# Threshold attention and a bilinear FFN: products in 128x64 array tiles rewritten as four 64x64 tiles

## The chip, the cores and the metric

One NeuronCore of a Trainium2 chip runs the whole program. The time is the device time of one execution in microseconds (us). The engines are PE (TensorE, matmul; PEld is its weight load), DVE (VectorE), ACT (ScalarE), POOL (GpSimd) and SP (SyncE, which here only issues DMAs). Matmuls write PSUM, eight banks of 128 partitions x 512 fp32 values; DVE and ACT carry results from there to SBUF.

## The reference

All arrays are fp32 but the weights w_a, w_b and w_out, which come as fp64. B = 8 batches, H = 8 heads, S = 576 positions, D = 64; the FFN has 4608 rows, a width of 512 and an inner width of 1536.

```
scores = q @ k.T / sqrt(64)                      # (8, 8, 576, 576)
thresh = max(scores, -1) - tau                   # tau = 0.02
scores = where(scores >= thresh, scores, -1e9)
attn   = exp(scores - max(scores, -1))
attn   = attn / (sum(attn, -1) + 1e-9)
o      = attn @ v                                # (8, 8, 576, 64)
x      = o.transpose(0, 2, 1, 3).reshape(4608, 512)
out    = ((x @ w_a) * (x @ w_b)) @ w_out         # (4608, 512)
```

## The kernel before

Heads are taken in pairs (32 pairs; the first head on partitions 0 to 63, the second on 64 to 127). A pair has five *units*: four of 128 queries for each of the two heads (u = 0 to 3) and one with the last 64 queries of both (u = 4, called NT). The loop over g (160 units, and three more rounds for what lags) writes out an order for every engine; `keep_order` at the end makes it binding. Each engine therefore does its work strictly in the order in which the loop issues it.

For one unit the loop issues, in this order:

1. `scores` (L308): PE multiplies qT by kT into two PSUM tiles of two banks each (`ps_sc`). qT and kT hold one head on each half of the partitions, so the two heads' products are two 64-row tiles of the array (64*128 in the profile: rows * columns). For u = NT a helper tile `q_diag` holds both heads' 64 queries with zeros elsewhere, written by POOL, and the product goes through `halves`, two tiles of 128 rows and 64 columns (128*64). DVE then takes the row maximum (L317), POOL the bias and threshold (L318, L319).
2. `turn_back`: SP fetches transposed weights of an older unit from a scratch in DRAM (wT).
3. `turn_blocks` for the unit before: DVE transposes in blocks of 32 (L398), SP writes them to the scratch. The first eight units are turned on PE instead (`turn_pe`, with PSUM tiles tp).
4. `weigh`: ACT takes exp (L330), DVE compares, multiplies and sums (L334).
5. `reciprocal` on DVE (L347), `normalise` on ACT (L353).
6. `advance(SPLIT * pace)`: a part of the FFN, see below.
7. every few units `weighted`: the product pv of attention weights and v for 256, 320 or 64 queries (`product`, L449), which lags three units behind. It has five slots of 128 keys; the fifth is shared by the two heads and uses `v_diag`, a tile with zeros written by POOL. ACT copies pv to the tile xT (L479, L487).
8. `advance((1 - SPLIT) * pace)`.

The FFN works on blocks of 256 rows, 18 of them. `ffn` is a generator: for each of 12 slices of 128 inner columns it makes two accumulation chains on PE, x @ w_a and x @ w_b (both called pab, four matmuls of 128 rows deep, each as two 128*64 tiles by `halves`, L457). ACT copies the first to a tile `a` (L517), DVE multiplies `a` with the second to h (L521). Then for each 128 of the 256 rows a chain po of 12 matmuls of 512 columns; ACT copies it to osb (L532) and SP stores it. In the profile each fp32 matmul is two records.

`advance` counts columns: it goes on with the generator until the pace of this unit is used up. Pace grows with the backlog of blocks (CATCH_UP). pv's columns are charged to the same account.

PSUM: four of eight banks are `ps_sc`, the other four are `ps_1`, a pool of four tiles of one bank that pab, po, pv and tp take in turn. A chain can start only when the tile that it takes has been read out.

SBUF: x blocks and raw fp64 weights share the tag xT (six tiles), h has twelve tiles. Weights are converted from fp64 to fp32 in 36 pieces of 128x512 in the first 160 us, spread over ACT, DVE and POOL.

Of the kernel before, what the change touches and what calls it, by code (L numbers as in the profile page):

```python
# [24 lines left out]
XT_BUFS = 6  # L25
W_BUFS = 4
WT_BUFS = 2
A_BUFS = 2
H_BUFS = 12
# [4 lines left out]
PACE_EARLY = 0.04  # L34

# [15 lines left out]
def kernel(  # L51
# [69 lines left out]
    ps_1 = pool("ps_1", 4, space=PSUM)  # L121
# [33 lines left out]
    wa_sb = const.tile([P, HP, DFF], FP32, name="wa_sb")  # L155
    wb_sb = const.tile([P, HP, DFF], FP32, name="wb_sb")
    wo_sb = const.tile([P, NF, DM], FP32, name="wo_sb")
    CW = DM
    pieces = []
    for f0 in range(0, DFF, CW):  # L160
        for c in range(HP):
            for dst, src in ((wa_sb, w_a), (wb_sb, w_b)):
                pieces.append((dst[:, c, f0:f0 + CW], src[c * P:(c + 1) * P, f0:f0 + CW]))
    for F in range(NF):
        pieces.append((wo_sb[:, F, :], w_out[F * P:(F + 1) * P, :]))
    NPIECES = len(pieces)
    raws, stages = {}, {}
    state = {"loaded": 0, "converted": 0, "rows": 0, "shared": 0}

    def load_weights(limit, engine=nc.sync):  # L170

        while len(raws) < limit and state["loaded"] < NPIECES:
            n = state["loaded"]
            raw = work.tile([P, CW, 2], U32, tag="xT", bufs=XT_BUFS, name="raw")
            engine.dma_start(raw.rearrange("p f w -> p (f w)"), pieces[n][1].bitcast(U32))
            raws[n] = raw
            state["loaded"] = n + 1
# [68 lines left out]
    q_diag = [const.tile([P, P], FP32, name=f"q_diag{i}") for i in range(1)]  # L246
    v_diag = [const.tile([P, 2, D], FP32, name=f"v_diag{i}") for i in range(2)]
    shared = []
    for t in q_diag + v_diag:
        nc.gpsimd.memset(t, 0.0)  # L250
# [15 lines left out]
    blocks, swaps, ready = [], {}, []  # L266
# [8 lines left out]
    def prep_pe(i, name):  # L275
# [3 lines left out]
        tps = []  # L279
        for c in range(2):  # L280
            tp = ps_1.tile([P, SH], FP32, tag="ps1", name="tp")
            for n in range(NR // 2):
                nc.tensor.transpose(tp[:, n * R:(n + 1) * R], m[:, c * (NR // 2) + n], ident[0:R, 0:R])
            tps.append(tp)
        prepared.setdefault(i, {})[name] = mT
        return mT, tps

    def prep_copy(mT, tps):
        for c, tp in enumerate(tps):
            nc.vector.tensor_copy(mT[:, c * SH:(c + 1) * SH], tp)  # L290

    def prep_tail(i):

        qT, qd = prepared[i]["q"], q_diag[0]
        for j in range(2):
            r = slice(j * D, (j + 1) * D)
            nc.gpsimd.tensor_copy(qd[r, j * TAIL:(j + 1) * TAIL], qT[r, MAIN:S])

    def scores(i, u):
        qT, kT = prepared[i]["q"], prepared[i]["k"]  # L300
        qd = q_diag[0]
        n = 2 if u < NT else 1
        sc = [ps_sc.tile([P, 2, 512], FP32, tag="sc", name="sc")[:, :, 0:SH] for _ in range(n)]
        for c in range(2):
            for j in range(n):
                if u < NT:
                    r = slice(j * D, (j + 1) * D)
                    nc.tensor.matmul(sc[j][:, c], qT[r, u * P:(u + 1) * P],  # L308
                                     kT[r, c * SH:(c + 1) * SH], start=True, stop=True)
                else:  # L310
                    halves(sc[j][:, c], qd, kT[:, c * SH:(c + 1) * SH], True, True)
# [51 lines left out]
    def turn_pe(i, u):  # L363
# [3 lines left out]
        turned[i, u, "pe"] = wT  # L367
        for j, w in enumerate(ws):
            tp = ps_1.tile([P, NT, P], FP32, tag="ps1", name="tp")
            for s in range(NT):  # L370
                c = TAIL * j + s * P
                nc.tensor.matmul(tp[:, s, :], w[:, c:c + P], dg[:, j], start=True, stop=True)
            nc.scalar.copy(wT[:, 5 * j:5 * j + NT], tp)
        tp = ps_1.tile([P, P], FP32, tag="ps1", name="tp")
# [15 lines left out]
    def turn_blocks(i, u):  # L390
# [20 lines left out]
        else:  # L411
            tb = work.tile([P, NB, Q], FP32, tag="tbt", bufs=1, name="tbt")
# [21 lines left out]
    def shared_slot(i):  # L434

        vm, vd = loaded[i]["v"], v_diag[state["shared"] % 2]
        state["shared"] += 1
        for j in range(2):
            r = slice(j * D, (j + 1) * D)
            nc.gpsimd.tensor_copy(vd[r, j], vm[r, NT])  # L440
        shared.append(vd)

    def product(wT, vm, n):
        vd = shared.pop(0)
        pv = ps_1.tile([P, n], FP32, tag="ps1", name="pv")
        for s in (NT, 0, 1, 2, 3):
            for j in range(2):
                k0 = NT if s == NT else 5 * j + s
                nc.tensor.matmul(pv[j * D:(j + 1) * D], vd[:, j] if s == NT else vm[:, k0], wT[:, k0, :],  # L449
                                 start=(s == NT), stop=(s == NT - 1))  # L450
        return pv

    def halves(out, stationary, moving, start, stop):

        for c in range(2):
            r = slice(c * D, (c + 1) * D)
            nc.tensor.matmul(out[r], stationary[:, r], moving, start=start, stop=stop)  # L457

    def weighted_unit(i, u):
# [5 lines left out]
        nc.scalar.copy(x_of[b, 0][:, hp, u * P:(u + 1) * P], pv)  # L465
        if hp == HP - 1:
            state["rows"] = u + 1
            if u == 0:
                blocks.append((x_of[b, 0], ("first", b, 0)))

    def weighted(i, h):
# [4 lines left out]
        if h < 2:  # L476
            if hp == 0:
                x_of[b, h] = work.tile([P, HP, HALF], FP32, tag="xT", bufs=XT_BUFS, name="xT")
            nc.scalar.copy(x_of[b, h][:, hp, :].rearrange("p (t i e) -> p i t e", t=2, e=Q),  # L479
                           pv[:, 0:HALF].rearrange("p (i t e) -> p i t e", t=2, e=Q))  # L480
            if hp == HP - 1:
                blocks.append((x_of.pop((b, h)), ("half", b, h)))
        if n % HALF:
# [3 lines left out]
            nc.scalar.copy(xtail_of[b // GT][:, hp, t * TAIL:(t + 1) * TAIL], pv[:, n - TAIL:n])  # L487
            del loaded[i], prepared[i]
            if hp == HP - 1 and t == GT - 1:
                blocks.append((xtail_of.pop(b // GT), ("tail", b - t, 0)))  # L490


    def ffn(xT, what):


        kind, b, h = what
        hs = []
        steps = [(F, 0, HALF) for F in range(NF)]
        if kind == "first":
            n = CW // P  # L500
            steps = [(F, c, c + P) for c in (0, P) for F in range(n)] + steps[n:]
        for F, c0, c1 in steps:
            while (state["converted"] < 2 * HP * (F * P // CW + 1)
                   or kind == "first" and state["rows"] * P < c1):
                yield 0
            fs = slice(F * P, (F + 1) * P)
            pab = []
            for w in (wa_sb, wb_sb):
                p = ps_1.tile([P, c1 - c0], FP32, tag="ps1", name="pab")
                for c in range(HP):  # L510
                    halves(p, w[:, c, fs], xT[:, c, c0:c1], c == 0, c == HP - 1)
                    if c < HP - 1:
                        yield c1 - c0
                pab.append(p)
                if w is wa_sb:
                    a = work.tile([P, c1 - c0], FP32, tag="a", bufs=A_BUFS, name="a")
                    nc.scalar.copy(a, p)  # L517
                    yield c1 - c0
            if c0 == 0:
                hs.append(work.tile([P, HALF], FP32, tag="h", bufs=H_BUFS, name="h"))  # L520
            nc.vector.tensor_tensor(hs[F][:, c0:c1], a, pab[1], op=ALU.mult)  # L521
            yield c1 - c0
        for u in range(2):
            po = ps_1.tile([P, DM], FP32, tag="ps1", name="po")
            for F in range(NF):
                while state["converted"] < NPIECES - NF + F + 1:
                    yield 0
                halves(po, hs[F][:, u * P:(u + 1) * P], wo_sb[:, F, :], F == 0, F == NF - 1)
                if F < NF - 1:
                    yield DM  # L530
            osb = work.tile([P, DM], FP32, tag="osb", bufs=OSB_BUFS, name="osb")
            nc.scalar.copy(osb, po)  # L532
# [7 lines left out]
            yield DM  # L540
# [169 lines left out]
```

## Time and profile before

| | |
|---|---|
| three runs | 1590.07, 1589.36, 1590.07 us; median 1590.07 |
| the profiled execution | 1591.21 us, of it 1589.4 us span |
| PE matmul records / weight loads | 11696 / 11696 |
| pab L457, 128x256 (all forms together) | 7040 records |
| po L457, 128x512 | 1728 records, 383.7 us |
| sc L308, 64x288 | 1024 records, 165.6 us |
| sc L457 on q_diag, 128x288 | 256 records, 36.5 us |
| pv L449 | 1440 records |
| ACT copy a, 128x256 (L517) | x212, mean 362 ns |
| ACT copy osb, 128x512 (L532) | x36, mean 570 ns |
| DVE h, 128x256 / 128x128 (L521) | x212, mean 416 ns / x8, mean 275 ns |
| POOL copies v_diag / q_diag | 34.4 / 14.9 us |
| DMA, instructions | 92 packets, 1.51 MB (queue q8) |
| swap<-tb, 288 KB; out, 256 KB: issue to landing | 5.1; 3.6 us (median) |

The busy times of engines are shares of the whole span and add up over stages with different limits. A matmul record lasts longer than its turn on the array, since matmuls are pipelined; the time that one costs is read from the distance of two starts. "Idle before" and its releaser tell what ended a wait.

### The profile page before, as it was taken

What the parts mean: (1) busy time and instruction counts of PE and PEld (TensorE: products, weight loads), DVE (VectorE), ACT (ScalarE), POOL (GpSimd) and SP (SyncE); (2) the same over time, 40 slices, a digit from 0 to 9 for tenths busy, and PEclk for the clock granted to TensorE, in tenths of its full rate; (3) what the DMA queues carried; (4) which work ended last, traced back from release to release, by engine and by line L of the source; (5) the groups of instructions that cost most, each with busy time, mean ns of one, the idle gap of its engine ahead of it and who ended that gap; (6) DMA issues with size and microseconds to landing.
All of it is one profiled execution on the core that took longest, in us unless ns stands there. A gap on an engine that the chain in (4) does not pass through costs nothing.

```text
span 1589.4 us, 29502 instructions
## 1 busy us (share of the span) xinstructions
PE 1523.8 (96%) x11696; PEld 852.8 (54%) x11696; DVE 828.3 (52%) x1810; ACT 592.3 (37%) x1045; POOL 250.3 (16%) x737
## 2 busy tenths in 40 slices
PE   6879999998999999999999999999999999999998
PEld 4655454644646464645555555555464546464654
DVE  6787465556655665564444654466545655430100
ACT  5766344433433443343332333343433333320010
POOL 4766111111111111110111111111101111000000
PEclk9989999999999999999999999999999999999999
DMA  9458877678767875785636956488656865550000
GB/s 226 156 144 221 168 139 175 142 150 185 170 150 145 183 177 132 148 173 129 141 82 123 186 128 143 104 181 163 145 108 148 181 149 133 111 127 14 1 14 14
DMA packets 621018, 218.99 MB, mean 138 GB/s; under 512 B 542544, under 2 KB 611664, under 8 KB 620880
## 3 DMA queue, kind: packets, MB, share of 16 engines
q1 hardware_dynamic: 618512, 216.52, 61.5%
q8 instruction: 92, 1.51, 0.4%
q10 hardware_dynamic: 2368, 0.59, 0.2%
q14 instruction: 46, 0.38, 0.1%
HBM read 127.40 MB, written 89.65 MB: 137 GB/s over the span
## 4 chain that ended last, share of the span: by engine, by line
PE 82%; DVE 6%; issue 3%; ACT 3%; DMA 3%; SPq 2%; POOL 1%; DVEq 0%; POOLq 0%; ACTq 0%
PE pab L457 41%; PE po L457 21%; PE pv L449 9%; PE sc L308 8%; PE sc L457 2%; DVE mx L317 1%; DVE w L334 1%; DMA wT<-swap 1%; SPq L137 1%; DVE tb L398 1%; ACT w L353 1%; SPq L420 1%; SPq L408 1%; POOL bias L318 1%; DMA km<-in_k_dram 1%
## 5 line engine op out<-in xcount | busy, mean ns | idle before, releaser
L317 DVE TENSOR_REDUCE mx<-sc 128x1 f32<-128x576 f32 x288 | 206.0, 752 | 379.1 <-PE sc L308 317.0
L457 PE MATMUL pab<-xT,wa_sb 128*64 128x256 f32 (+1 forms) x3136 | 376.2, 378 | 19.0 <-ACT a L517 13.1
L457 PE MATMUL po<-wo_sb,h 128*64 128x512 f32 x1728 | 383.7, 594 | 0.3 <-ACT a L517 0.3
L457 PE MATMUL pab<-xT,wb_sb 128*64 128x256 f32 (+1 forms) x3136 | 375.2, 377 | 2.3 <-ACT a L517 1.3
L330 ACT ACTIVATE w<-sc,bias,scalars 128x576 f32<-128x576 f32 x288 | 226.8, 827 | 368.7 <-POOL bias L318 368.4
L353 ACT ACTIVATE w<-w,rcp 128x576 f32<-128x576 f32 x272 | 197.7, 768 | 274.6 <-DVE rcp L347 274.6
L457 PEld LDWEIGHTS pab<-xT,wa_sb 128*64 128x64 f32 x3136 | 219.9, 138 | 146.2 <-issue 20.1
L457 PEld LDWEIGHTS pab<-xT,wb_sb 128*64 128x64 f32 x3136 | 220.0, 137 | 121.6 <-issue 15.0
L318 POOL TENSOR_SCALAR bias<-mx,scalars 128x1 f32<-128x1 f32 x288 | 89.9, 312 | 1134.0 <-DVE mx L317 1125.4
L521 DVE TENSOR_TENSOR h<-a,pab 128x256 f32<-128x256 f32 (+1 forms) x220 | 89.0, 411 | 312.5 <-PE pab L457 170.5
L457 PEld LDWEIGHTS po<-wo_sb,h 128*64 128x64 f32 x1728 | 120.8, 137 | 228.7 <-issue 221.4
L334 DVE SCALAR_TENSOR_TENSOR w<-sc,thr,w 128x576 f32<-128x576 f32 x288 | 221.7, 802 | 10.1 <-POOL thr L319 2.4
L308 PE MATMUL sc<-kT,qT 64*128 64x288 f32 x1024 | 165.6, 439 | 9.9 <-DVE w L334 6.2
L398 DVE STREAM_TRANSPOSE tb<-w 128x576 f32<-128x576 f32 x240 | 171.2, 752 | 0.0
L449 PE MATMUL pv<-wT,vm 128*64 128x256 f32 (+3 forms) x1152 | 143.6, 393 | 0.0
L308 PEld LDWEIGHTS sc<-kT,qT 64*128 64x128 f32 x1024 | 91.9, 190 | 82.9 <-issue 59.5
L517 ACT COPY a<-pab 128x256 f32<-128x256 f32 (+1 forms) x220 | 73.3, 358 | 117.5 <-PE pab L457 107.0
L449 PEld LDWEIGHTS pv<-wT,vm 128*64 128x64 f32 x1152 | 85.6, 143 | 45.4 <-issue 2.1
L479 ACT COPY xT<-pv 128x256 f32<-128x256 f32 x60 | 22.3, 372 | 147.2 <-PE pv L449 147.2
L449 PE MATMUL pv<-wT,v_diag 128*64 128x256 f32 (+3 forms) x288 | 45.9, 397 | 18.0 <-issue 9.0
L319 POOL TENSOR_SCALAR thr<-mx,scalars 128x2 f32<-128x2 f32 (+1 forms) x160 | 47.8, 299 | 0.0
L457 PE MATMUL pab<-xt,wa_sb 128*64 128x256 f32 x384 | 45.8, 380 | 0.7 <-ACT a L517 0.7
(58 smaller groups left out, 655.7 us busy)
## 6 DMA issues: line engine op xcount, KB each, us to landing
swap<-tb SPq DMA_DIRECT2D x240, 288.0 KB, 5.1
wT<-swap SPq DMA_DIRECT2D x28, 1440.0 KB, 7.1
wT<-swap SPq DMA_DIRECT2D x32, 1152.0 KB, 6.2
vm<-in_v_dram SPq DMA_DIRECT2D x32, 288.0 KB, 4.2
swap<-tbt SPq DMA_DIRECT2D x128, 72.0 KB, 2.2
out_dram<-osb SPq DMA_DIRECT2D x32, 256.0 KB, 3.6
qm<-in_q_dram SPq DMA_DIRECT2D x112, 72.0 KB, 3.3
km<-in_k_dram SPq DMA_DIRECT2D x112, 72.0 KB, 4.5
```

The lines of the kernel that those rows point to most:

```text
L308: nc.tensor.matmul(sc[j][:, c], qT[r, u * P:(u + 1) * P], kT[r, c * SH:(c + 1) * SH], start=True, stop=True)
L317: nc.vector.tensor_reduce(mx[:, c], sc[j], axis=AX.XY, op=ALU.max)
L318: nc.gpsimd.tensor_scalar(bias[:, c], mx[:, c], e_nscale, None, op0=ALU.mult)
L319: nc.gpsimd.tensor_scalar(thr[:, 0:n], mx[:, 0:n], cut, None, op0=ALU.subtract)
L330: nc.scalar.activation(w.rearrange("p (c k) -> p c k", c=2), s, AF.Exp, bias=bias[:, j:j + 1], scale=e_scale)
L334: nc.vector.scalar_tensor_tensor(out=wv, in0=s, scalar=thr[:, j:j + 1], in1=wv, op0=ALU.is_ge, op1=ALU.mult, accum_out=sums[:, j:j + 1])
L353: nc.scalar.activation(w, w, AF.Copy, scale=rcp[:, j:j + 1])
L398: nc.vector.transpose(tb[:, j * NB:(j + 1) * NB, (u % 2) * Q:(u % 2 + 1) * Q], w.rearrange("p (n e) -> p n e", e=Q))
L449: nc.tensor.matmul(pv[j * D:(j + 1) * D], vd[:, j] if s == NT else vm[:, k0], wT[:, k0, :], start=(s == NT), stop=(s == NT - 1))
L457: nc.tensor.matmul(out[r], stationary[:, r], moving, start=start, stop=stop)
L517: nc.scalar.copy(a, p)
L521: nc.vector.tensor_tensor(hs[F][:, c0:c1], a, pab[1], op=ALU.mult)
```

## The change

Every product on PE, outside the transposes of the first units, becomes a set of matmuls of 64 rows and 64 columns, four of which lie side by side on the array (two row halves x two column halves). Row halves write different PSUM banks.

- `ps_1` with its four one-bank tiles becomes `ps_2` with two tiles of two banks; `banks(n, name)` hands out a tile of [P, 2, n].
- The weights wa_sb and wb_sb are laid out anew: row half r holds the columns r * 256 to r * 256 + 255 of each group of 512, for all 512 inputs, in eight chunks of 64. A chain now makes 128 inner columns on each of two banks (256 in all) from eight chunks; bank r needs chunks of x that lie on row half r. For four of the chunks these are x itself, for the other four a copy xs of x with its partition halves exchanged. There are six steps of two chains a block, where there were twelve.
- `swapped` makes xs by two DMAs on SP. A finished block waits in `complete` until `swap_blocks` at the start of the next unit allots xs, issues the DMAs and queues the block. The first block is swapped in two parts by `weighted_rows`.
- ACT copies the first chain's two banks straight to h (512 columns), DVE multiplies the second in place. The tile `a` is gone; h has six tiles of twice the size.
- po and pv split the contraction over the row halves, so their two banks are partial sums: `join` copies one (ACT) and adds the other (DVE).
- `q_diag` and `v_diag`, their memsets and POOL copies are gone.
- `make_room` goes on with the FFN before a pv until no chain is open or the open one has at least 1024 columns behind and before it.
- The pieces of w_a and w_b are loaded with two DMAs each; XT_BUFS is 7; the tile tbt uses the ring w.

```diff
-XT_BUFS = 6
+XT_BUFS = 7
-A_BUFS = 2
-H_BUFS = 12
+H_BUFS = 6
+ROOM = 1024
...
-    ps_1 = pool("ps_1", 4, space=PSUM)
+    ps_2 = pool("ps_2", 2, space=PSUM)
+    def banks(n, name):
+        return ps_2.tile([P, 2, 512], FP32, tag="ps2", name=name)[:, :, 0:n]
...
+    CH = CW // 2
+    NG = DFF // CW
+    wa_sb = const.tile([P, NG, H, CH], FP32, name="wa_sb")
+    wb_sb = const.tile([P, NG, H, CH], FP32, name="wb_sb")
...
         for c in range(2):
-            for j in range(n):
-                if u < NT:
+            for t in range(n):
+                for j in range(2):
                     r = slice(j * D, (j + 1) * D)
-                    nc.tensor.matmul(sc[j][:, c], qT[r, u * P:(u + 1) * P],
+                    q0, to = (u * P + t * D, slice(t * D, (t + 1) * D)) if u < NT else (MAIN, r)
+                    nc.tensor.matmul(sc[j if u < NT else 0][to, c], qT[r, q0:q0 + D],
                                      kT[r, c * SH:(c + 1) * SH], start=True, stop=True)
-                else:
-                    halves(sc[j][:, c], qd, kT[:, c * SH:(c + 1) * SH], True, True)
...
+    def join(out, lo, hi):
+        nc.scalar.copy(out, lo)
+        nc.vector.tensor_tensor(out, out, hi, op=ALU.add)
...
-        pv = ps_1.tile([P, n], FP32, tag="ps1", name="pv")
+        pv = banks(n, "pv")
         for s in (NT, 0, 1, 2, 3):
-            for j in range(2):
-                k0 = NT if s == NT else 5 * j + s
-                nc.tensor.matmul(pv[j * D:(j + 1) * D], vd[:, j] if s == NT else vm[:, k0], wT[:, k0, :],
-                                 start=(s == NT), stop=(s == NT - 1))
+            for r in range(2):
+                rows = slice(r * D, (r + 1) * D)
+                for j in ((r,) if s == NT else range(2)):
+                    k0 = NT if s == NT else 5 * j + s
+                    nc.tensor.matmul(pv[j * D:(j + 1) * D, r], vm[rows, k0], wT[rows, k0],
+                                     start=(s == (NT if j == r else 0)), stop=(s == NT - 1))
...
+    def swapped(x, xs, c0, c1):
+        for r in range(2):
+            nc.sync.dma_start(xs[r * D:(r + 1) * D, :, c0:c1], x[(1 - r) * D:(2 - r) * D, :, c0:c1])
+    def swap_blocks():
+        while complete:
+            x, what = complete.pop(0)
+            xs = work.tile([P, HP, HALF], FP32, tag="xT", bufs=XT_BUFS, name="xS")
+            swapped(x, xs, 0, HALF)
+            blocks.append(((x, xs), what))
...
             for w in (wa_sb, wb_sb):
-                p = ps_1.tile([P, c1 - c0], FP32, tag="ps1", name="pab")
-                for c in range(HP):
-                    halves(p, w[:, c, fs], xT[:, c, c0:c1], c == 0, c == HP - 1)
+                pab = banks(c1 - c0, "pab")
+                for k in range(H):
+                    for r in range(2):
+                        rows = slice(r * D, (r + 1) * D)
+                        moving = (x if k < HP else xs)[rows, k % HP, c0:c1]
+                        for c in range(2):
+                            nc.tensor.matmul(pab[c * D:(c + 1) * D, r],
+                                             w[rows, f // n, k, fs + c * D:fs + (c + 1) * D], moving,
+                                             start=(k == 0), stop=(k == H - 1))
...
                 if w is wa_sb:
-                    a = work.tile([P, c1 - c0], FP32, tag="a", bufs=A_BUFS, name="a")
-                    nc.scalar.copy(a, p)
+                    nc.scalar.copy(ht, pab)
+                else:
+                    nc.vector.tensor_tensor(ht, ht, pab, op=ALU.mult)
...
-                halves(po, hs[F][:, u * P:(u + 1) * P], wo_sb[:, F, :], F == 0, F == NF - 1)
+                ht = hs[F // (2 * n) * n + F % n][:, F // n % 2]
+                for r in range(2):
+                    rows = slice(r * D, (r + 1) * D)
+                    for c in range(2):
+                        t0 = u * P + c * D
+                        nc.tensor.matmul(po[c * D:(c + 1) * D, r], ht[rows, t0:t0 + D], wo_sb[rows, F, :],
+                                         start=(F == 0), stop=(F == NF - 1))
...
-            nc.scalar.copy(osb, po)
+            join(osb, po[:, 0], po[:, 1])
...
+    def make_room():
+        while running["rest"] and not (running["done"] >= ROOM and running["rest"] >= ROOM):
+            owed = running["owed"]
+            running["owed"] = 0.0
+            advance(1)
+            running["owed"] += owed - 1
...
         if BY_PE <= n < len(units) and part(*units[n]):
+            make_room()
             weighted(*part(*units[n]))
```

## The prediction

> **What bounds the kernel now.** I read the page first: busy times, and the chain that ended last.
>
> ```profile
> span 1589.4 us, 29502 instructions
> ...
> PE 1523.8 (96%) x11696; PEld 852.8 (54%) x11696; DVE 828.3 (52%) x1810; ACT 592.3 (37%) x1045; POOL 250.3 (16%) x737
> ...
> PE 82%; DVE 6%; issue 3%; ACT 3%; DMA 3%; SPq 2%; POOL 1%; DVEq 0%; POOLq 0%; ACTq 0%
> ```
>
> PE is busy 96% of the span and makes up 82% of the chain. By stage (columns: busy time of PE, PEld, DVE, ACT, POOL, the granted clock, DMA share, GB/s):
>
> ```profile
> 60.00:160.00 100.00, 81.99 (x751) 55.81 (x749) 81.36 (x154) 66.15 (x127) 69.53 (x98) 0.93 0.64 177
> 160.00:400.00 240.00, 225.13 (x1720) 123.11 (x1718) 139.12 (x310) 93.64 (x157) 30.59 (x121) 0.98 0.77 161
> 400.00:800.00 400.00, 396.40 (x2986) 215.25 (x2984) 227.02 (x506) 155.33 (x261) 48.61 (x190) 1.00 0.70 153
> ...
> 1440.00:1500.00 60.00, 60.00 (x464) 33.15 (x462) 5.05 (x12) 5.27 (x13) 0.00 (x0) 1.00 0.03 10
> ```
>
> Up to 160 us four engines share the limit; then PE is the bound alone, to the end. So after 160 us PE's own seconds count, and whatever makes it wait. Two units of the timeline show both (start, length, engine, line):
>
> ```profile
> 1003.50 0.44 PE L449 MATMUL pv<-wT,vm 128*64 128x320 f32 x2
> ...
> 1003.87 1.24 PE L308 MATMUL sc<-kT,qT 64*128 64x288 f32 x8
> ...
> 1005.04 1.08 PE L457 MATMUL pab<-xT,wb_sb 128*64 128x256 f32 x8
> ...
> 1005.96 1.90 PE L457 MATMUL pab<-xT,wa_sb 128*64 128x256 f32 x16
> ...
> 1007.68 1.90 PE L457 MATMUL pab<-xT,wb_sb 128*64 128x256 f32 x16
> ...
> 1012.53 1.24 PE L308 MATMUL sc<-kT,qT 64*128 64x288 f32 x8
> ...
> 1018.25 0.17 DVE L347 RECIPROCAL rcp<-sums 128x2 f32<-128x2 f32 x1
> ...
> 1018.46 1.44 ACT L353 ACTIVATE w<-w,rcp 128x576 f32<-128x576 f32 x2 [1.85 <-DVE rcp L347]
> ...
> 1019.80 0.62 ACT L517 COPY a<-pab 128x256 f32<-128x256 f32 x2
> ...
> 1021.95 1.14 PE L457 MATMUL sc<-kT,q_diag 128*64 128x288 f32 x8
> ...
> 1022.92 6.18 PE L457 MATMUL po<-wo_sb,h 128*64 128x512 f32 x28
> ```
>
> First, the **step**. A chain of 16 matmul records starts every 1.72 us (1005.96, 1007.68): 8 pairs, two column halves at once, 0.216 us a pair. Second, the **switch**. The last pv pair (320 columns, 0.269 us by the same rate) ends its turn at 1003.77; scores start at 1003.87, 0.10 late. Their four pairs at 0.2425 (288 columns) end at 1004.84; pab starts at 1005.04, 0.20 late. Its four pairs (0.863) end at 1005.90; the next chain starts 0.06 late. So one change to 64-row tiles and back costs 0.35 us. The scores on q_diag, in 128*64 tiles like the FFN, take 1022.92 - 1021.95 = 0.97: four pairs, nothing lost. Third, the **run-ahead**. ACT takes the pab copies only behind normalise: 7.3 us after the scores began. PE meanwhile lives on free PSUM. The view of waits, from 160 to 1440 us:
>
> ```profile
> PE pab L457 <- ACT a L517: 7.8, 12, 1.3
> ```
>
> PE's wait for the copies is only 7.8 us, 12 times: the run-ahead is just long enough.
>
> **The change, part by part.** *Array work: nothing.* Four 64x64 tiles do in one step what two 128x64 tiles did: pab 18 blocks x 192 steps x 0.216 = 746 us, po 864 x 0.43 = 371, scores 640 x 0.2425 = 155, pv about 150; the same number of steps as before. The trace has column halves at once (pab) and row halves at once (sc), never four; that they combine is the first thing taken on trust. Bounds: all four together, 0; two at a time, twice those 1422 us. I take 0, as each kind of pairing alone loses nothing. Matmul records nearly double (pab 7040 to 14080, po 1728 to 3456, sc 1024 to 2048, pv 1440 to 2592), so a pab step must issue 8 instructions in 0.216 us. The densest row is the 64-column pv, behind a wait that had emptied PE's queue:
>
> ```profile
> 204.82 0.58 PEld L449 LDWEIGHTS pv<-wT,vm 128*64 128x64 f32 x16
> 204.87 0.67 PE L449 MATMUL pv<-wT,vm 128*64 128x64 f32 x16
> ```
>
> 16 loads and 16 matmuls in some 0.45 us of starts (0.58 less one load's 0.14), 14 ns an instruction; 8 take 0.11. Issue costs 0, at most (if that rate does not last) the 54 ns of steady pab: another 0.216 a pab step.
> [...]
> [...]
>
> *Switches removed.* 128 units have qT scores. The first 16 lie in the stage that PE does not bound. 112 x 0.35 = **-39 us** (if each lost only its 0.20 on the way out, -22).
>
> *PSUM ring: 4 x 1 bank becomes 2 x 2 banks.* A chain now takes 16 steps, 3.46 us. Before, PE could finish the open chain and three more (5.2 us) without an evacuation; now the open chain and one (3.46 us). After the scores (0.97), PE needs the first buffer back at 0.97 + rest + 3.46. For an a chain it is back when normalise has ended (1018.46 + 1.44 - 1012.53 = 7.37, less 0.1 for the switch) and the 512-column copy is done (0.57, the osb row): 7.8. For a b chain, when reciprocal has ended (5.89 - 0.1) and the product of 512 is done (0.41 at 256 and 0.27 at 128 give an estimate of 0.70): 6.45. With the rest spread evenly over 0 to 3.46 the mean wait is (everything behind the chain waits with it on PE, the next scores too) (7.8 - 4.43)²/6.92 = 1.6 and (6.45 - 4.43)²/6.92 = 0.6, mean 1.1 us. The FFN is in pab for 2/3 of its time and 11/12 of the chains are followed by one that matters: 140 units give 86 x 1.1 = 95 us. Counting the columns through the pacing loop unit by unit, with each unit's own reciprocal and normalise times, gives less, since make_room sets the rest and the paces differ: 67 us in 50 units. The same count for the kernel before gives 17 us; the wait view shows 7.8 idle, as the records of matmuls hide part. So **+50 us**, between +23 (67 scaled by 7.8/17, less 8) and +87 (95 - 8).
>
> *Joins and larger evacuations.* ACT copies of pab halve in number (0.57 for 2 x 0.36). DVE gets an add for each product: 60 x 0.41, 36 x 0.70 and 40 small ones, 57 us, less 13 saved on h: hidden in DVE's 48% idle; the pv add ends about 1.0 us after pv, before the scores' reduction could start (1.2). Without cover it would be 0.4 us for each of 60. At the very end one add stands bare: **+1**.
>
> *Swapped x.* Two DMAs a block on SP, behind turn_back; they wait for the join, and the swap writes, loads and stores queued behind them come later in the unit anyway. xs is read 4 steps of k (1.73 us) into a chain. Where a block is queued that is hidden. By the column count the queue is empty at three starts (units 19, 31, 43): join 1.0 + landing 3.6 to 5.1 (256 KB stores, 288 KB swaps) - 0.97 - 1.73 gives 2 to 3.5 each: **+8** (0 to 11).
>
> *Before 160 us.* The unit's DVE has the join ahead of its select (8 times, up to 0.6), two waits for swapped rows of about 4, and turn_pe has two buffers where it had four (about 7 by the same count): **+15** (0 to 30). Weights as 24 x 2 DMAs of half the rows: SP's issue, 24 x 0.4 us over 100 us, hidden. The memsets, q_diag and v_diag copies taken from POOL (49 us of 16% busy): 0.
>
> **Sum.** 1589.4 - 39 + 50 + 1 + 8 + 15 = 1624 of span. The profiled run was 1591.21, 1.8 above its span and 1.1 above the median of 1590.07; so about **1625 us**.
>
> **Rivals.** (1) *The switches win.* Faster: if the chains fall so that waits grow by less than 15 us of the forecast's 50, 39 outweighs the rest. For it: removed losses are read off directly, the waits only counted, and make_room exists to place the products; against it: a buffer freed at 7.8 cannot serve a PE that wants it at 4.4 plus the rest. With the waits' low end and the sums of start and queue at 0, 1590 - 39 + 23 + 1 = 1575; with no new wait at all 1552. Chance 0.30, range 1552 to 1586.
> (2) *Four tiles do not share the array or its issue.* At two at a time, +1422; if only issue or instruction fetch drags (92 packets of 16 KB before, 256 instructions each, which last 6.9 us instead of 13.8 against landings of 2.2 to 7.1), 10% of the 746 us of pab gives 1700. Chance 0.07.
> (3) *It is a draw*: +39 against -39, within 0.2% (3.2 us, about what this kernel's runs can tell): 0.05.
> Forecast 1595 to 1680: 0.58. Together: faster 0.30, same 0.05, slower 0.65. The range of 8 in 10 reaches into (1): 1560 to 1680; the forecast's own is 1597 to 1670.
>
> **What would show it.** Right: steps of 0.216 in pab with four starts in each; sc records of 64*64 with no 0.1 before and 0.2 behind; "PE pab <- ACT" grown from 8 to some 50 to 70 us with PE's idle time in the steady stages; PE busy about 1480. Wrong: pab steps above 0.22 (rival 2); pab waits below 25 us (rival 1); DVE's add or the swap's DMA as the releaser in steady units.

## The result and the profile after

The changed kernel takes 1690.93 us (median of 4 runs, 1685.82 to 1691.39), the kernel before 1590.07 (4 runs, 1589.36 to 1591.19): a ratio of 1.0626, 95% interval 1.0605 to 1.0648. It is slower, as forecast, but by 101 us and not by 35, and 11 us above the forecast's 1595 to 1680.

The page of the changed kernel: span, busy times, and the chain that ended last by engine and by line.

```profile
span 1688.9 us, 50940 instructions
...
PE 1521.3 (90%) x22640; PEld 1054.1 (62%) x22640; DVE 869.5 (51%) x1828; ACT 591.3 (35%) x935; POOL 208.7 (12%) x526
...
PE 58%; DVE 18%; DMA 7%; SPq 7%; issue 5%; ACT 4%; POOL 1%; DVEq 0%; ACTq 0%; POOLq 0%
```

PE's share of the chain falls from 82% to 58%; DVE, DMA and SP's queue come in. PE was the bound, and it now waits for others. By stage (the columns are those of the view before):

```profile
60.00:160.00 100.00, 67.31 (x1204) 52.89 (x1206) 62.56 (x111) 51.98 (x97) 52.17 (x62) 0.81 0.53 134
160.00:400.00 240.00, 210.86 (x3074) 140.75 (x3068) 135.76 (x293) 89.66 (x139) 32.82 (x84) 0.94 0.69 149
400.00:800.00 400.00, 361.62 (x5284) 246.22 (x5280) 234.68 (x508) 152.53 (x228) 36.30 (x129) 0.97 0.75 160
...
1560.00:1620.00 60.00, 60.00 (x939) 50.45 (x934) 5.50 (x8) 4.27 (x8) 0.00 (x0) 1.00 0.03 11
```

From 400 to 800 us PE was busy for 396.40 of 400 us; now it is for 361.62. At the end, where only the FFN is left, it is busy all the time as before. The losses lie where attention and FFN share PE, most densely in the start (60 to 160 us). The granted clock is lower too: 0.81 where it was 0.93, 0.94 where it was 0.98.

What PE waited for over the whole run (us, times, longest):

```profile
PE pab L529 <- DMA xS<-xT: 41.8, 5, 12.3
PE pab L529 <- ACT h L535: 31.0, 17, 2.9
PE pab L529 <- DVE h L537: 17.1, 17, 3.9
...
PE pv L450 <- ACT h L535: 5.5, 3, 2.0
...
PE po L549 <- ACT h L535: 4.1, 4, 1.9
...
PE pv L450 <- DVE h L537: 3.4, 3, 1.7
```

Two groups: five long waits for the exchanged x, and many short ones for the PSUM ring, 61.1 us in the other five rows. Counted from the matmul records, the time in which none runs grew from 53.7 to 155.1 us (+101.4). The work done while the clock was at 0.50 lost 37.8 us to it (half of PE's busy time there), against 16.3 before (+21.5). What remains, above all matmul time at full clock, fell by 23.4 us. Together that is the 99.5 us of span.

**Four tiles share the array.** The timeline in the pure FFN stage (start, length, engine, line, records of one group):

```profile
1562.29 0.38 PE L529 MATMUL pab<-xT,wb_sb 64*64 64x256 f32 x2
1562.41 0.41 PE L529 MATMUL pab<-xS,wa_sb 64*64 64x256 f32 x2
1562.50 0.38 PE L529 MATMUL pab<-xT,wb_sb 64*64 64x256 f32 x2
1562.62 0.38 PE L529 MATMUL pab<-xS,wa_sb 64*64 64x256 f32 x1
1562.66 1.67 PE L529 MATMUL pab<-xT,wb_sb 64*64 64x256 f32 x25
...
1564.39 1.67 PE L529 MATMUL pab<-xS,wb_sb 64*64 64x256 f32 x25
...
1566.11 1.67 PE L529 MATMUL pab<-xT,wa_sb 64*64 64x256 f32 x25
```

Half a chain (eight steps) takes 1564.39 - 1562.66 = 1.73 us, or 0.216 a step with four matmuls in it. That is the step of before: the array work neither gains nor loses, and the second rival falls.

**A ring wait**, in a unit of the steady stage:

```profile
648.66 0.17 DVE L350 RECIPROCAL rcp<-sums 128x2 f32<-128x2 f32 x1
648.86 1.44 ACT L356 ACTIVATE w<-w,rcp 128x576 f32<-128x576 f32 x2 [1.85 <-DVE rcp L350]
650.21 0.56 ACT L535 COPY h<-pab 128x512 f32<-128x512 f32 x1
...
650.82 1.96 PE L529 MATMUL pab<-xT,wa_sb 64*64 64x256 f32 x32 [1.90 <-ACT h L535]
```

ACT idles 1.85 us until the reciprocal comes, normalises for 1.44, and only then copies the chain that PE needs out of the way. PE waits 1.90 us. This is the wait that the forecast had counted.

**A wait for the exchanged x**, 424.6 to 436.9 us. First the timeline, then clock and busy time by stretch:

```profile
421.57 4.37 SPq L141 DMA_DIRECT2D qm<-in_q_dram  x4
425.98 0.50 SPq L569 DMA_DIRECT2D out_dram<-osb  x1
426.64 0.38 SPq L435 DMA_DIRECT2D wT<-swap  x1
427.07 1.52 SPq L457 DMA_DIRECT2D xS<-xT  x2
428.63 6.46 SPq L141 DMA_DIRECT2D km<-in_k_dram  x4
```

```profile
423.03 0.22 DVE L440 TENSOR_TENSOR xt<-xt,pv 128x64 f32<-128x64 f32 x1 [0.28 <-ACT xt L439]
```

```profile
436.88 2.16 PE L529 MATMUL pab<-xS,wa_sb 64*64 64x256 f32 x14 [12.32 <-DMA xS<-xT]
```

```profile
425.00:428.40 3.40, 0.00 (x0) 0.00 (x0) 3.28 (x9) 1.01 (x3) 0.23 (x1) 1.00 1.01 192
428.40:442.10 13.70, 5.22 (x48) 4.90 (x52) 0.00 (x0) 1.97 (x3) 0.00 (x0) 0.50 0.77 165
442.00:460.00 18.00, 16.90 (x300) 13.98 (x292) 10.36 (x22) 5.39 (x8) 1.69 (x6) 1.00 0.50 100
```

x was joined at 423.25. SP was then issuing four loads, a store and a fetch, and the exchange's first DMA went out 3.82 us later, at 427.07. It landed at 436.83, 9.76 us after its issue; the share of the DMA engines stands at 1.01 just before and at 0.77 during the wait. For 13.7 us from 428.4 on the clock stands at 0.50, so the first matmuls behind the wait run at half speed too: eight steps take 3.41 us from 438.21 on, 0.43 a step of four matmuls, against 0.216 once the clock is back.

In the start the place in SP's queue costs more. From 96.18 to 110.53 SP issues five loads of raw weights, and PE waits 11.36 us (from 103.83) for the exchange behind them. What SP itself waited for, from 94 to 112 us, and then from 54 to 62 us:

```profile
SPq L195 <- DVE low L227: 14.5, 4, 5.1
```

```profile
SPq L457 <- DVE low L227: 3.4, 1, 3.4
```

L227 is the last instruction that reads a raw weight tile, and raw weights, x and its exchanged copy take their tiles from one ring (the tag xT). So SP stands until a conversion frees a tile: once in the loads ahead of the exchange, once in the exchange itself.

### The profile page after: what moved, and what is told of

Same layout as the page of the kernel before. It is cut to its first block, busy times and chain, and to the rows that moved or that the text cites. A ratio compares the mean times of both kernels' runs of the same rounds, so it can differ in the third digit from the quotient of the medians.

```text
span 1688.9 us, 50940 instructions
## 1 busy us (share of the span) xinstructions
PE 1521.3 (90%) x22640; PEld 1054.1 (62%) x22640; DVE 869.5 (51%) x1828; ACT 591.3 (35%) x935; POOL 208.7 (12%) x526
## 4 chain that ended last, share of the span: by engine, by line
PE 58%; DVE 18%; DMA 7%; SPq 7%; issue 5%; ACT 4%; POOL 1%; DVEq 0%; ACTq 0%; POOLq 0%
PE pab L529 25%; PE po L549 18%; PE pv L450 7%; PE sc L313 7%; DVE mx L320 5%; DVE w L337 5%; DVE tb L402 3%; SPq L412 3%; SPq L141 2%; DMA swap<-tb 2%; ACT w L356 2%; DMA xS<-xT 2%; SPq L424 1%; DVE low L227 1%; DMA wT<-swap 1%
## 5 line engine op out<-in xcount | busy, mean ns | idle before, releaser
L549 PE MATMUL po<-wo_sb,h 64*64 64x512 f32 x3456 | 406.0, 592 | 7.7 <-ACT h L535 4.1
L549 PEld LDWEIGHTS po<-wo_sb,h 64*64 64x64 f32 x3456 | 180.9, 133 | 183.5 <-issue 144.6
L529 PE MATMUL pab<-xS,wa_sb 64*64 64x256 f32 (+1 forms) x3520 | 256.1, 383 | 41.8 <-DMA xS<-xT 41.8
L529 PE MATMUL pab<-xT,wa_sb 64*64 64x256 f32 (+1 forms) x3136 | 220.2, 384 | 33.5 <-ACT h L535 29.7
L529 PE MATMUL pab<-xS,wb_sb 64*64 64x256 f32 (+1 forms) x3520 | 247.1, 374 | 0.0
L313 PE MATMUL sc<-kT,qT 64*64 64x288 f32 x2304 | 232.5, 420 | 14.6 <-DVE sums L348 5.7
L529 PE MATMUL pab<-xT,wb_sb 64*64 64x256 f32 (+1 forms) x3136 | 217.7, 382 | 20.2 <-DVE h L537 16.6
L529 PEld LDWEIGHTS pab<-xS,wa_sb 64*64 64x64 f32 x3520 | 175.4, 137 | 80.7 <-DMA xS<-xT 39.7
L450 PE MATMUL pv<-wT,vm 64*64 64x320 f32 (+3 forms) x2592 | 182.3, 396 | 25.8 <-issue 8.9
L529 PEld LDWEIGHTS pab<-xS,wb_sb 64*64 64x64 f32 x3520 | 170.9, 133 | 35.0 <-issue 0.6
```

Of the source, the lines that this page charges most:

```text
L313: nc.tensor.matmul(sc[j if u < NT else 0][to, c], qT[r, q0:q0 + D], kT[r, c * SH:(c + 1) * SH], start=True, stop=True)
L450: nc.tensor.matmul(pv[j * D:(j + 1) * D, r], vm[rows, k0], wT[rows, k0], start=(s == (NT if j == r else 0)), stop=(s == NT - 1))
L529: nc.tensor.matmul(pab[c * D:(c + 1) * D, r], w[rows, f // n, k, fs + c * D:fs + (c + 1) * D], moving, start=(k == 0), stop=(k == H - 1))
L549: nc.tensor.matmul(po[c * D:(c + 1) * D, r], ht[rows, t0:t0 + D], wo_sb[rows, F, :], start=(F == 0), stop=(F == NF - 1))
```

## The experiments

Each is compared with the kernel before, run on the same chip. The median of the kernel before lies between 1590.07 and 1592.01 us there, so differences between two rows can be off by some 2 us.

| run | median us | ratio to before, 95% interval |
|---|---|---|
| changed kernel | 1690.93 | 1.0626 [1.0605, 1.0648] |
| e1 no exchange | 1634.14 | 1.0274 [1.0256, 1.0293] |
| e2 before, with the ring alone | 1643.12 | 1.0327 [1.0312, 1.0343] |
| e3 scores on row tiles | 1705.61 | 1.0722 [1.0697, 1.0747] |
| e4 exchange on POOL's queue | 1676.87 | 1.0540 [1.0522, 1.0558] |
| e5 no join add | 1677.88 | 1.0552 [1.0531, 1.0574] |
| e6 early copy of a | 1639.65 | 1.0300 [1.0274, 1.0327] |
| e7 exchange by POOL copies | 1657.61 | 1.0417 [1.0395, 1.0439] |
| e8 = e7 + early evacuation of a and b | 1589.07 | 0.9991 [0.9980, 1.0002] |
| e9 = e8 + first exchange early | 1578.06 | 0.9915 [0.9902, 0.9929] |
| e10 before, with early evacuation | 1570.11 | 0.9867 [0.9853, 0.9880] |
| e11 = e8 with scores on row tiles | 1615.59 | 1.0153 [1.0139, 1.0167] |
| e12 = e9, every chain finished early | 1572.12 | 0.9882 [0.9864, 0.9900] |

**e1: no exchange.**

```diff
-            xs = work.tile([P, HP, HALF], FP32, tag="xT", bufs=XT_BUFS, name="xS")
-            swapped(x, xs, 0, HALF)
-            blocks.append(((x, xs), what))
+            blocks.append(((x, x), what))
...
```

> This kernel is the changed one, but every chunk is multiplied with x as it was before the exchange: no exchanged copy is made, no DMA for it, no wait for it (the exchange is left out of what is computed). My theory: the waits 'pab L529 <- DMA xS<-xT' (41.8 us of the changed kernel's profile) go, and with them some 8 to 12 us of work at half clock behind them: 1635 to 1645 us. Rival, that the ring of PSUM and the array set the time and the waits for the exchanged x would only move to the next waits: 1680 us or more.

Measured: 1634.14, 57 us less than the changed kernel and just under the theory's range. The waits for xS are gone, the loss to half clock falls from 37.8 to 21.5 us (more than the 8 to 12 expected), and the ring's waits stay about as they were:

```profile
PE pab L524 <- ACT h L530: 34.1, 18, 3.1
PE pab L524 <- DVE h L532: 17.7, 17, 3.9
```

41.8 of waits and 16.3 of half clock make 58. The two losses lie one after the other: taking one away hardly feeds the other.

**e2: the ring alone, in the kernel before.** Tiles of 128x64, no exchange, no joins; two PSUM tiles of two banks, chains of two slices, copies and products of 512 columns, and `make_room`, which comes with them.

```diff
-    ps_1 = pool("ps_1", 4, space=PSUM)
+    ps_2 = pool("ps_2", 2, space=PSUM)
...
-        steps = [(F, 0, HALF) for F in range(NF)]
+        steps = [(f, 0, HALF) for f in range(NF // 2)]
...
+                pab = banks(c1 - c0, "pab")
+                for k in range(2 * HP):
+                    c, e = k // 2, k % 2
+                    fs = slice((2 * f + e) * P, (2 * f + e + 1) * P)
+                    halves(pab[:, e], w[:, c, fs], xT[:, c, c0:c1], c == 0, c == HP - 1)
...
```

> This is the kernel before (128x64 tiles, no exchange, no adds of two banks), with one thing of the change: the ring of accumulators is two tiles of two banks in place of four of one, with chains of two slices each, evacuated 512 columns at a time. My theory: the ring's run-ahead is worth 50 us (the waits of pab for ACT and DVE grow from 8 to about 55 us), plus a few of half clock: 1640 to 1655 us. Rival, that the four tiles, the exchange and the adds carry the whole loss: 1590 to 1600 us.

Measured: 1643.12, 52 us over the kernel before. Without one four-tile product the ring shows the same waits:

```profile
PE pab L459 <- ACT h L520: 27.0, 16, 5.4
PE pab L459 <- DVE h L522: 13.0, 13, 3.7
...
PE pab L459 <- ACT osb L533: 8.4, 6, 1.9
...
PE po L459 <- ACT h L520: 6.0, 4, 3.0
```

The theory holds. As a mark for the end of the start I take the 31st row maximum on DVE, which starts at 151.35 us in the kernel before: there e2 is 12.3 us late. So some 39 of the 52 us lie behind the start, where the forecast had its +50, and 6.8 us of the whole are half clock (23.1 us of loss against 16.3).

**e3: the scores back on 64x128 row tiles.**

```diff
-            for t in range(n):
-                for j in range(2):
-                    r = slice(j * D, (j + 1) * D)
-                    q0, to = (u * P + t * D, slice(t * D, (t + 1) * D)) if u < NT else (MAIN, r)
-                    nc.tensor.matmul(sc[j if u < NT else 0][to, c], qT[r, q0:q0 + D],
+            for j in range(2):
+                r = slice(j * D, (j + 1) * D)
+                q0, to = (u * P, slice(0, P)) if u < NT else (MAIN, r)
+                nc.tensor.matmul(sc[j if u < NT else 0][to, c], qT[r, q0:q0 + (P if u < NT else D)],
```

> The changed kernel with the scores of the transposed part back on 64x128 row tiles, as before the change: the switches of the tile mode around them come back. My theory: 112 units by 0.28 to 0.35 us, 32 to 39 us more than the changed kernel: 1723 to 1730 us, with about 0.1 us ahead of and 0.2 us behind each such group. Rival, that the switches had no price of their own: 1691 us, within 5.

Measured: 1705.61, only 15 us more; neither the theory's 32 to 39 nor the rival's 0. The page says where the rest went:

```profile
PE 1551.0 (91%) x21616; PEld 941.9 (55%) x21616; DVE 870.5 (51%) x1828; ACT 592.1 (35%) x935; POOL 207.7 (12%) x526
```

PE's busy time grew by 29.7 us, although the loss to half clock fell from 37.8 to 32.5; without half clock it grew by 35.0, as the theory has it. But the time without a matmul fell by 16.4 (155.1 to 138.7). My reading was that a PE that takes longer over the scores comes later to a PSUM tile that is late anyway, so that half of the price is free where the ring binds. e11 tests this reading.

**e4 and e7: the transport of the exchange.** e4 moves the two DMAs to POOL's queue; e7 replaces them by two copies on GpSimd (the edit shown).

```diff
-            nc.sync.dma_start(xs[r * D:(r + 1) * D, :, c0:c1], x[(1 - r) * D:(2 - r) * D, :, c0:c1])
+            nc.gpsimd.tensor_copy(xs[r * D:(r + 1) * D, :, c0:c1], x[(1 - r) * D:(2 - r) * D, :, c0:c1])
```

> The changed kernel with the DMAs of the exchange issued from POOL's queue and not SP's. My theory: what made the exchanged x late was mostly its place in SP's queue, behind outputs, weights and loads that wait; so the part of 41.8 us that is lateness of issue goes and the landing of 2.5 to 5 us at each start remains: 20 to 30 us less, 1660 to 1670 us. Rival, that the landing itself is the wait (the queue is free in time, the transfer is slow): 1685 us or more.

> The changed kernel with the exchanged x made by two GpSimd copies across the partition halves in place of two DMAs. From POOL's 128x512 rows (610 to 650 ns) a copy of 64x1024 is estimated at 1.25 us, the pair at 2.5 us, on an engine that idles 88% of the span. My theory: queue place and landing of the DMA go, 2 to 3 us remain at each start: the wait for xS falls from 41.8 to 10 to 15 us, and the half clock behind it: 1645 to 1655 us. Rival, that the wait is for the join of x itself and not for the transport, so that it stays: 1680 us or more.

Measured: e4 1676.87 (14 us less), e7 1657.61 (33 less). Both fall between theory and rival, nearer to the theory. The wait for xS in e4, and in e7 with its copies (busy time, mean ns | idle before):

```profile
PE pab L529 <- DMA xS<-xT: 33.0, 8, 10.6
```

```profile
PE pab L529 <- POOL xS L457: 18.7, 8, 8.1
```

```profile
L457 POOL COPY xS<-xT 64x1024 f32<-64x1024 f32 x30 | 31.1, 1036 | 29.9 <-DVE xT L440 28.2
```

On POOL's queue the wait of 12.32 us became 5.16 and 1.24 for the second DMA. The two waits of the start stayed, 6.62 and 10.64 us: at 112.10 the exchange goes out right behind POOL's weight conversions. So e4 changes the queue but does not free the exchange of its place in one. A copy takes 1.04 us, where a DMA of the same size took a median of 4.7 us from issue to landing in the changed kernel. What is left in e7 are mostly the two waits of the first block (4.86 and 8.13 us), which e9 explains.

**e5: no add in the join.**

```diff
     def join(out, lo, hi):
         nc.scalar.copy(out, lo)
-        nc.vector.tensor_tensor(out, out, hi, op=ALU.add)
```

> The changed kernel without the DVE add that joins the sums of two banks (the second bank's sums are left out of x and of the output rows; the ACT copy stays). The runs so far leave about 5 to 8 us for it: no exchange 1634 = before 1590 + ring 52 - switches 15 + the rest 7. My theory: the adds lie in DVE's idle time but for the start, 5 to 8 us less than the changed kernel: 1683 to 1686 us. Rival, that the adds stand ahead of the transposes and masks on DVE and carry what the start lost: 20 us or more, 1671 us or less.

Measured: 1677.88, 13 us less, between the two. It isn't the start: at the 31st row maximum the changed kernel is 30.0 us late and this one 29.1. In the changed kernel the rows in which PE waits for the add itself hold 6.2 us for xT (in the start) and 4.6 us for osb (behind it); here they are gone, with 2.5 us of waits for the copies in their place. The loss to half clock is higher in this run (45.0 us), so more must have been gained elsewhere; where, was not tried.

**e6: early evacuation.** A chain of w_a that is nearly done is finished in the program before reciprocal and normalise are issued. PE's order is the same; ACT's copy moves into the 1.85 us for which ACT idled above.

```diff
+EARLY = "a"
+EARLY_COLS = 1024
...
+    def finish(kinds, most):
+        while running["rest"] and running["rest"] <= most and running["chain"] in kinds:
+            owed = running["owed"]
+            running["owed"] = 0.0
+            advance(1)
+            running["owed"] += owed - 1
...
             weigh(i, u)
+            if g > BY_PE:
+                finish(EARLY, EARLY_COLS)
```

> The changed kernel, where a chain of w_a that has at most 1024 columns to go is finished in the program right behind the weighing of a unit, so that ACT's copy of it (ht <- pab) stands ahead of ACT's normalising, which waits for DVE's sums and reciprocal; TensorE's order stays. My theory: the ring waits 'pab <- ACT h' (31.0 us) exist because the copy queues behind a waiting normalise; they fall to about 15, 12 to 20 us less in time: 1671 to 1679 us. Rival, that the waits only move (the normalised weights come later, DVE's multiplications take over as releaser): 1691 us, within 5.

Measured: 1639.65, 51 us less, far more than the 12 to 20 expected. The waits for ACT all but vanish:

```profile
PE pab L532 <- DVE h L540: 18.5, 18, 3.9
...
PE pab L532 <- ACT h L538: 2.3, 2, 1.6
PE po L553 <- ACT h L538: 2.2, 2, 1.2
...
PE pv L452 <- ACT h L538: 1.6, 1, 1.6
```

40.6 us of waits for ACT's h (31.0 + 5.5 + 4.1) became 6.1, and the loss to half clock fell by 11.7 us: in the changed kernel six of the waits for ACT's h behind 460 us are followed by 3.4 us at 0.50 each. I had expected half of the pab waits to stay and had left pv, po and the clock out.

**e8: both remedies**, with the products of w_b finished early too (chains with at most 1536 columns to go).

> Both: the exchange by GpSimd copies, and chains of w_a and w_b with at most 1536 columns to go finished right behind the weighing, so that ACT's copy stands ahead of the normalising and DVE's multiplication ahead of the reciprocal. My theory (the parts add): 1650 less 15 to 30: 1620 to 1635 us, still slower than before (1590), since the ring of two keeps part of its waits. Rival, that early multiplications hold up the reciprocal and so the weights: 1650 us or more.

Measured: 1589.07, 31 us better than the lower bound of the theory and equal to the kernel before. The remedies of e6 and e7 gave 51 and 33; all together give 102, and the other 18 are not split between the chains of w_b, the higher limit and the two remedies helping each other. The loss to half clock is 12.2 us, less than before the change.

**e9: the first exchange early.** In e8 the largest wait left was in the start. The join of x (DVE), the POOL queue and PE:

```profile
100.64 0.27 DVE L442 TENSOR_TENSOR xT<-xT,pv 128x128 f32<-128x128 f32 x1
```

```profile
102.28 1.27 POOL L240 TENSOR_TENSOR wa_sb<-wa_sb,low 128x512 int32<-128x512 int32 x1
...
107.12 1.71 POOL L240 TENSOR_TENSOR wa_sb<-wa_sb,low 128x512 int32<-128x512 int32 x1
108.89 1.28 POOL L459 COPY xS<-xT 64x512 f32<-64x512 f32 x2
```

```profile
109.55 2.43 PE L532 MATMUL pab<-xS,wa_sb 64*64 64x128 f32 x30 [7.87 <-POOL xS L459]
```

x is there at 100.91; the copies stand behind the unit's weight conversions and run at 108.89. e9 issues them head pair by head pair, right behind each join.

```diff
...
+        join(x, pv[:, 0], pv[:, 1])
+        for r in range(2):
+            nc.gpsimd.tensor_copy(xs[r * D:(r + 1) * D], x[(1 - r) * D:(2 - r) * D])
...
```

> The previous kernel (exchange by GpSimd copies, early evacuation: 1589.1 us), where the exchange of the first rows is made head pair by head pair right behind each join, and not for all four behind the unit's weight conversions, which stand in POOL's queue ahead of it (in its trace the joined x was there at 54.1 and 100.9 us, the copies ran at 62.0 and 108.9 us, and TensorE waited 4.86 and 7.87 us). My theory: both waits go, 10 to 12 us, and 2 to 4 us of half clock behind them: 1573 to 1579 us, faster than before (1590.5). Rival, that the next thing of the start (weights, weighting on DVE) is due at the same moment: 1585 us or more.

Measured: 1578.06, as expected. At the 31st row maximum this kernel is 0.4 us ahead of the kernel before.

**e10: early evacuation in the kernel before.**

```diff
             weigh(i, u)
+            if g > BY_PE:
+                finish()
```

Here `finish` goes on while a chain of pab is open.

> The kernel before with the early evacuation alone: an open chain of pab is finished in the program right behind the weighing of a unit. Its ring of four single banks hides the copies (7.8 us of waits for ACT from 160 us on). My theory: at most those 8 us, 1582 to 1592 us, so the gain of the early evacuation belongs to the ring of two. Rival, that early evacuation is worth 30 us or more to any version, and the four tiles nothing: 1560 us or less.

Measured: 1570.11, 21 us less than the kernel before by the ratio, more than the 8 expected and less than the rival's 30. I had counted only the rows that name ACT. The kernel before, and then this one, over the whole run:

```profile
PE pab L457 <- ACT a L517: 15.1, 14, 4.6
PE pv L449 <- issue: 9.0, 9, 1.8
```

```profile
PE pab L457 <- ACT a L519: 5.3, 2, 4.5
...
PE pv L449 <- issue: 1.5, 2, 1.3
```

The row "pv <- issue" goes with the copies too, so it was mostly the same wait under another name.

**e11: the switches once more, in e8**, where few ring waits are left. The edit is that of e3.

> The kernel with copies and early evacuation (1589.1 us) with the scores of the transposed part back on 64x128 row tiles. On the changed kernel the same edit cost 15 us and not the 32 to 39 expected. My theory: there the ring's waits took up half of it (TensorE's idle time fell by 16 us as its work grew); here few such waits are left, so nearly the whole price shows: 25 to 32 us more, 1614 to 1621 us. Rival, that the switches are worth only 15 us: 1604 us, within 4.

Measured: 1615.59, 26 us more than e8, as expected. But the reading of e3 does not follow:

```profile
PE 1533.2 (95%) x21616; PEld 938.9 (58%) x21616; DVE 871.9 (54%) x1828; ACT 591.8 (37%) x935; POOL 245.4 (15%) x564
```

Against e8, PE's busy time grew by 43.2 us (from 1490.0), without half clock by 35.4, the same as in e3. The time without a matmul fell by 14.1 us (82.3 to 68.2), nearly as much as in e3, though few ring waits were left to absorb anything. What differs is half clock: its loss fell by 5.3 us in e3 and rose by 7.8 here. So PE's busy time grows by 35 us in both kernels, some 15 us of it are made up by shorter idles in both, and the price in time was 15 or 26 us with the clock. Which idles shrink, and why, stays open; part of it may be records drawn over time in which PE waited, which no run shows.

**e12: every open chain of up to 2048 columns finished early**, those of w_out too, in e9.

> The best version of the four tiles so far (1578.1 us), which now finishes any open chain of up to 2048 columns behind the weighing, those of w_out too. Its remaining ring waits are pab and pv for ACT h and DVE h (17.6 us over the run). My theory: half of these go, 5 to 9 us less: 1569 to 1573 us, about the kernel before with early evacuation (1570.1). Rival, that the longer chains hold up ACT's normalising and DVE's reciprocal as much as they give: 1576 us or more.

Measured: 1572.12, 6 us less than e9. The intervals of e12 and e10 overlap: with early evacuation on both sides, the four tiles give no gain that these runs can tell from none.

## Why the prediction was wrong, point by point

| term | forecast us | measured us | by |
|---|---|---|---|
| array work of four tiles | 0 | 0 (0.216 a step) | trace |
| switches removed | -39 | -15 here, -26 in e8 | e3, e11 |
| PSUM ring | +50 | +52 | e2 |
| joins | +1 | +13 | e5 |
| exchange of x | +8, and part of the +15 | +57 | e1 |
| rest of the start | the rest of the +15 | within the terms above | e1, e2, e9 |
| half clock behind idles | no term | +21.5, within the terms above | trace |

The measured terms add up to 107, the difference is 101. The terms of e1 and e2 hold their part of the start. Behind the start, by the spans, the exchange is 39.0 us (57.4 less 18.4) where the forecast had 8, and the ring 39.4 (51.7 less 12.3) where it had 50.

*Exchange, the step that failed.* The forecast said "where a block is queued that is hidden" and gave each of three starts 2 to 3.5 us, for join and landing alone. The three starts came, but PE waited 8.83, 3.74 and 12.32 us at them, not 8 us in all. Of the first block's two waits "of about 4" one was 5.58 and the other 11.36. What was left out is what stands ahead of the exchange: SP issues in the order of the program, and from the join of x to the issue it took 6.72, 7.24, 5.96, 0.92 and 3.82 us at the five waits. The landings took 2.46, 4.58, 4.61, 4.58 and 9.76 us, the last far above the 3.6 to 5.1 assumed. Place and landing weigh about the same (24.7 and 26.0 us in all), and no run separates them in full. The forecast did say that the DMAs issue behind turn_back, but asked only what they delay, not what delays them; and it called SP's issue of the weights hidden, while SP stood there until conversions freed tiles.

*Half clock, a term that was missing.* The stages of before showed a granted clock of 0.93 and 0.98 and the sum made nothing of it. In the trace of the changed kernel the clock stands at 0.50 for 13.7 us from 3.8 us into the idle of 12.32 us on. Shorter idles are followed by the slow clock too (2.02 us at 1182.9, with 3.4 us at 0.50 from 1186.1). Each long wait has to be priced with the slow work behind it: 41.8 us of waits cost 57.

*Ring, right in mechanism and about in size.* e2 shows the wait that was forecast, with some 39 us behind the start (50, between 23 and 87), half clock included. The forecast's sign, "PE pab <- ACT" at 50 to 70 us, did not come: that row shows 31.0, as the rest stands with DVE's h and with pv and po (61.1 together). The run-ahead of before was called just long enough by its 7.8 us; e10 gained 21 us there, so the ring of four was already losing more than that row said. (The wait for a b chain adds up to 6.49, not 6.45, which changes nothing.) The step of the array stayed at 0.216 us, and the ring of two tiles alone cost 52 us (e2).

*Switches, about right on PE, too large in time.* 112 units at 0.35 us were to give 39 us. Put back, the row tiles add 35.0 and 35.4 us to PE's busy time without half clock (e3, e11), 0.31 a unit. But the forecast took a gain on PE for a gain of the kernel at full price: PE idled 16.4 and 14.1 us less with the row tiles, and the time moved by 15 and 26.

*Joins, too small.* "Hidden in DVE's 48% idle" missed 12 us (e5). An engine with idle time can still be late: PE waited 10.8 us in rows that name the add. Where the rest of the 13 us comes from stays open.

*Start.* Forecast +15, measured +30 at the 31st row maximum. Without the exchange it is 11.6 (e1), with the ring alone 12.3 (e2). About 18 are the exchange, and the ring alone accounts for the rest.

*PE busy* was to be about 1480 and is 1521.3, the half clock among it; in e9, where half clock costs 13.6 us, it is 1488.7.

*Rivals.* The first had the ring's waits grow by less than 15 us; the ring alone cost 52. The second fell with the 0.216 us step, the third with the ratio.

## What to carry to other kernels

A halved ring of accumulators was paid in run-ahead (52 us, e2): before changing tile shapes, ask which evacuation stands behind a waiting instruction, and move that first; here a few lines gave 51 us to the changed kernel and 21 to the one before (1570.11; no version measured faster). A transfer put on SP's busy queue cost its place in it (24.7 us over five waits), so list what stands ahead of it at the moment it is needed, and what that in turn waits for. Price an idle on the matmul engine together with the slow clock behind it (here 41.8 us of waits cost 57). And when a reading explains one pair of runs, take the second pair apart in the same way before calling it confirmed: e3 and e11 differ by the clock, not by the ring.

## What the runs showed of the hardware

- In the changed kernel the clock stood at 0.50 for 3.4 us from 1186.1, behind an idle of 2.02 us at 1182.9, and for 3.4 us from 807.3, at the end of one of 2.75 us at 805.0; around an idle of 2.50 us at 755.4 it stayed at 1.00.
- Four tiles drift apart: in the FFN lines above the starts come 0.12, 0.09, 0.12 and 0.04 us after one another, tiles of one chain half running beside those of the next, and the rate is still 0.216 us a step.
- A GpSimd copy of 64x1024 fp32 across the partition halves takes 1.04 us (e7); a DMA of the same size took a median of 4.7 us from issue to landing in the changed kernel, and 9.76 in the longest wait.
- A wait can stand in the profile under "issue": in the kernel before, 7.5 of 9.0 us of "pv <- issue" went away with the early PSUM copies (e10).
- Score products on 64x128 row tiles among four-tile products add 35 us to PE's busy time without half clock over 112 units, in two kernels (e3, e11).
